# Five split pairs instead of four in the middle blocks of an attention and GeGLU kernel, with weight sums made earlier on GpSimd

## Chip, core and metric

The kernel runs on one core of a Trainium2 chip. The engines are TensorE (matmuls), VectorE (DVE), ScalarE (ACT), GpSimd (POOL) and SyncE (SP, which issues DMAs). The metric is the device time of one execution in microseconds; the median of three runs stands for a kernel.

## What is computed

For each of 8 batches, linear attention over 8 heads, 576 tokens and 64 values per head; its output, 4608 rows of 512, goes through a GeGLU layer of 1536 hidden columns:

```python
q_s = softmax(q, axis=-1); k_s = softmax(k, axis=2)
kv  = einsum('bhsd,bhse->bhde', k_s, v)
x   = einsum('bhsd,bhde->bhse', q_s, kv)      # then (B*S, H*D)
out = (gelu(x @ w_gate) * (x @ w_val)) @ w_out
```

All arrays are float32 outside; the matmuls use float16 operands and add up in float32.

## The kernel before

**Blocks.** Each batch gives a block of 512 rows; the 64 rows left over in each batch are gathered (`xtr`) into a ninth block. The order is 0 to 6, then block 8 (the gathered rows), then block 7 (`order`, L531). While TensorE works on the gate and value products of one block, the other engines do the softmax of the next batch, and DMAs load the one after.

**Plain tiles.** The 1536 hidden columns are 12 tiles of 128. A plain tile is 8 matmuls with 512 columns, 4 for the gate and 4 for the value, then a Gelu on ScalarE and a product on VectorE into `ht`. In the middle blocks `half` (L620) does the gate or the value of one tile.

**Pairs.** Tiles k and k+3 can be done together by a scheme of seven products in place of eight (Strassen's, in Winograd's form): the contraction, the tiles and the rows are halved, and sums of weights (`sum_wgv`, L580) and of x (`sum_x`, L589) replace some operands. A product is 4 matmuls of 256 columns. `pair_step` (L630) does a pair k in four steps, written k.1 to k.4:

- k.1: product 1 into bank `pa`; ScalarE copies `pa` into bank `pb`; product 5 into bank `pc`; a snapshot s5 of `pc`, on ScalarE, or on VectorE in the last two blocks (`snap`).
- k.2: product 6 on top of `pa`, snapshot s2 on ScalarE; product 3 on top of `pc`; VectorE adds `pc` and s2 into buffer `cc` (`add`).
- k.3: product 7 on top of `pa`, VectorE adds `pa` and s5 into `cc`; product 2 on top of `pb`; a half Gelu on ScalarE and a half product on VectorE write the lower half of tile k (`final`); `upper` puts a Gelu over half of `cc` on ScalarE, and GpSimd multiplies into the upper halves of tiles k and k+3 (L653).
- k.4: product 4 on top of `pa`, then `final` for the lower half of tile k+3.

The eight PSUM banks are handed out in a ring. In blocks from 3 on, pairs take two `cc` buffers in turn; in block 2 one buffer serves all.

**The written order.** The order within a block is written out by hand as strings (L611 to L615): `1.2` is a step of a pair, `8g` a half, and letters are work that rides along (`ride`, from `plan`): `a` and `n` start the softmax sums of the next batch's q (VectorE reductions; GpSimd products with `a`), `m` is two more GpSimd products of that softmax (L250), `t` transposes by DMA, `l` loads, `s0`, `s1`, `u0`, `u1` are sums of `ht` (`sum_h`, L566) for the next stage, `w` and `x` sums of weights for pair 6. Each engine runs its instructions in the order in which this code emits them. Block 2 has three pairs (`THREE`), blocks 3 to 6 have four (`FOUR`: 0, 6, 1, 2), blocks 8 and 7 all six (`SIX`). A function put into `live["late"]` is emitted after the next step.

**Out product.** `out_strassen` (L728) multiplies `ht` with `w_out` in the same way, from block 1 on: seven products of 12 matmuls with 256 columns, with the last step .4 of the block's last pair inside product 1. Sums of `w_out` (`tw`) and of `ht` (`sh`) lie in six buffers of a pool `wstp`, which first staged the float32 weights: these buffers have 2048 float16 places each, of which the sums use 1536.

**Weight sums.** Those of pairs 0 to 2 are made in blocks 0 and 1, those of pair 6 in block 2 on GpSimd, those of pairs 7 and 8 by VectorE in the out products of blocks 3, 4 and 6 (L999).

Of the kernel before, what the change touches and what calls it, by code (L numbers as in the profile page):

```python
# [9 lines left out]
f32 = mybir.dt.float32  # L10
f16 = mybir.dt.float16
# [7 lines left out]
def kernel(  # L19
# [12 lines left out]
    B, H, S, D = q.shape  # L32
    C = H * D
    F = moe_w_gate.shape[1]
    P = 128
    HP = H // 2
    NFI = F // P
# [11 lines left out]
    NO = NFI // 2  # L49
# [3 lines left out]
    wstp = ctx.enter_context(tc.tile_pool(name="wstp", bufs=6))  # L53
    att = ctx.enter_context(tc.tile_pool(name="att", bufs=2))
    ffn = ctx.enter_context(tc.tile_pool(name="ffn", bufs=4))
# [49 lines left out]
    ek_b, eq_b, v16_b = [], [], []  # L105
# [7 lines left out]
    ws = {(nm, 0): const.tile([P, 3, 2, NO // 2 * P], f16, name=f"ws{nm}") for nm in "gv"}  # L113
# [7 lines left out]
    for i, nm in enumerate("gv"):  # L121
        n = 3 * NO * P
        ws[(nm, 1)] = kt1[:, i * n:(i + 1) * n].rearrange("p (s c f) -> p s c f", s=3, c=2)
    cc_b = eq_b[1].rearrange("p n c -> p (n c)").bitcast(f32)[:, 0:1024].rearrange(
        "p (i t r) -> p i t r", i=2, t=2)

    xs_b = [xs, ld_b["v"][0].rearrange("p h x -> p (h x)").bitcast(f16)[:, 0:2048].rearrange(
        "p (i c r) -> p i c r", i=4, c=2)]
# [44 lines left out]
    wst = {}  # L173
# [373 lines left out]

    tw = {}  # L550

    def sum_w(i, eng="dve"):
        t = wstp.tile([P, NO, 256], f16, name=f"tw{i}", tag="wst")
        b11, b12 = wo_sb[:, 0:NO, 0:256], wo_sb[:, 0:NO, 256:512]
        b21, b22 = wo_sb[:, NO:NFI, 0:256], wo_sb[:, NO:NFI, 256:512]
        a, b = {1: (b12, b11), 2: (b22, tw.get(1)), 3: (b22, b12), 4: (b21, tw.get(2))}[i]
        (nc.gpsimd if eng == "pool" else nc.vector).tensor_tensor(out=t, in0=a, in1=b, op=ALU.subtract)
        tw[i] = t

    sh = {}  # L560

    def make_s():
        for i in (1, 2):
            sh[i] = wstp.tile([P, NO, 256], f16, name=f"sh{i}", tag="wst")

    def sum_h(j0, j1, which, eng="dve"):  # L566
        step = 1 if j1 - j0 == 2 else NO // 2
# [9 lines left out]

    def sum_wgv(nm, i, k=0, n=NO // 2, eng="dve"):  # L580
        w = wg_sb if nm == "g" else wv_sb
        lo, hi = slice(k * P, (k + n) * P), slice((k + NO // 2) * P, (k + NO // 2 + n) * P)
        a11, a21, a12, a22 = w[:, 0:2, lo], w[:, 0:2, hi], w[:, 2:4, lo], w[:, 2:4, hi]
        t = [ws[(nm, k // NO)][:, j, :, k % NO * P:(k % NO + n) * P] for j in range(3)]
        o, a, b, op = {1: (t[0], a21, a22, ALU.add), 2: (t[1], t[0], a11, ALU.subtract),
                       3: (a21, a11, a21, ALU.subtract), 4: (t[2], a12, t[1], ALU.subtract)}[i]
        (nc.gpsimd if eng == "pool" else nc.vector).tensor_tensor(out=o, in0=a, in1=b, op=op)
# [6 lines left out]

    def product_gv(i, ps, xt, k, first):
        lo, hi = slice(k * P, (k + 1) * P), slice((k + NO // 2) * P, (k + NO // 2 + 1) * P)
        sl = slice(k % NO * P, (k % NO + 1) * P)
        xs = xs_b[xt is st.get((B - 1, "xt"))]
        for t, w, nm in ((0, wv_sb, "v"), (1, wg_sb, "g")):
            ss = ws[(nm, k // NO)]  # L600
            for c in range(2):
                a = {1: w[:, c, lo], 2: w[:, 2 + c, lo], 3: ss[:, 2, c, sl], 4: w[:, 2 + c, hi],
                     5: ss[:, 0, c, sl], 6: ss[:, 1, c, sl], 7: w[:, c, hi]}[i]
                x = {1: xt[:, c, 0:256], 2: xt[:, 2 + c, 0:256], 3: xt[:, 2 + c, 256:512],
                     4: xs[:, 3, c], 5: xs[:, 0, c], 6: xs[:, 1, c], 7: xs[:, 2, c]}[i]
                nc.tensor.matmul(ps[:, t], a, x, start=(first and t == 0 and c == 0), stop=(c == 1),  # L606
                                 skip_group_check=True)

    THREE = ("a 6g l 6v 0.1 9g 0.2 9v w 0.3 7g 0.4 n m 1.1 t 7v 1.2 10g 1.3 s0 10v 1.4 2.1 u0 8g 2.2 8v"  # L611
             " 2.3 s1 11g u1 2.4 11v x")
    FOUR = ("a 7g l 7v n 0.1 6.1 0.2 6.2 0.3 6.3 m 10g 0.4 6.4 1.1 t 10v 1.2 s0 8g u0 1.3 8v 1.4 2.1"
            " 11g s1 2.2 11v 2.3")
    SIX = ("0.1 6.1 0.2 6.2 0.3 6.3 0.4 1.1 6.4 7.1 s0 1.2 7.2 1.3 u0 7.3 1.4 2.1 7.4 8.1 2.2"  # L615
           " 8.2 2.3 s1 8.3 2.4")
    steps = {b: (SIX if b >= B - 1 else THREE if b == 2 else FOUR).split() for b in range(2, B + 1)}
    live = {}

    def half(b, xt, c, nm):  # L620
# [9 lines left out]
    def pair_step(b, xt, k, i):  # L630
        def final(ps, fi):
            gl = ffn.tile([P, 256], f32, name="glq", tag="gl")
            nc.scalar.activation(out=gl, in_=ps[:, 1], func=ACTF.Gelu)  # L633
            nc.vector.scalar_tensor_tensor(out=ht[:, fi, 0:256], in0=ps[:, 0], scalar=_H_SCALE,  # L634
                                           in1=gl, op0=ALU.mult, op1=ALU.mult)
            let_go(ps)

        def snap(ps, dve=False):
            sn = ffn.tile([P, 2, 256], f32, name="snq", tag="snq")
            if dve:  # L640
                nc.vector.tensor_scalar(out=sn, in0=ps, scalar1=_H_SCALE, scalar2=None, op0=ALU.mult)
            else:
                nc.scalar.activation(out=sn, in_=ps, func=ACTF.Copy, scale=_H_SCALE)  # L643
            return sn

        def add(o, ps, sn):
            nc.vector.scalar_tensor_tensor(out=o, in0=ps, scalar=_H_SCALE, in1=sn,
                                           op0=ALU.mult, op1=ALU.add)

        def upper(cc):  # L650
            nc.scalar.activation(out=cc[:, :, 1], in_=cc[:, :, 1], func=ACTF.Gelu,  # L651
                                 scale=1.0 / _H_SCALE)
            (nc.vector if k == NFI - NO // 2 - 1 else nc.gpsimd).tensor_tensor(  # L653
                out=ht[:, k:k + NO // 2 + 1:NO // 2, 256:512], in0=cc[:, :, 0], in1=cc[:, :, 1],
                op=ALU.mult)

        if i == 1:
            live["odd"] = odd = b > 2 and not live.get("odd", True)
            cc = cc_b if odd else ffn.tile([P, 2, 2, 256], f32, name="cc", tag="cc", bufs=1)
            pa = big([P, 2, 256], f32, "pga", True)  # L660
            product_gv(1, pa, xt, k, True)
            pb = big([P, 2, 256], f32, "pgb", True, True)
            nc.scalar.copy(out=pb, in_=pa)  # L663
            pc = big([P, 2, 256], f32, "pgc", True)
            product_gv(5, pc, xt, k, True)
            live[k] = [cc, pa, pb, pc, snap(pc, b >= B - 1)]
            return
        cc, pa, pb, pc, s5 = live[k]
        if i == 2:
            product_gv(6, pa, xt, k, False)  # L670
            s2 = snap(pa)
            product_gv(3, pc, xt, k, False)
            add(cc[:, 0], pc, s2)
            let_go(pc)
        elif i == 3:
            product_gv(7, pa, xt, k, False)
            add(cc[:, 1], pa, s5)
            product_gv(2, pb, xt, k, False)
            final(pb, k)
            if k == NFI - NO // 2 - 1:  # L680
                live["late"] = lambda: upper(cc)
            else:
                upper(cc)
        else:
            product_gv(4, pa, xt, k, False)
            if steps[b] and steps[b][0].endswith(".1"):
                live["late"] = lambda: final(pa, k + NO // 2)
            else:
                final(pa, k + NO // 2)
# [38 lines left out]
    def out_strassen(b, last):  # L728
        yo = [yop.tile([P, 2, C], f32, name="yo", tag="yo") for _ in range(2)]
        c = (slice(0, 256), slice(256, 512))  # L730
# [31 lines left out]
        four = 2 < b < B - 1  # L762
# [3 lines left out]
            pair_step(b, get_x(b), NO // 2 - 1, 4)  # L766
            product(1, ps["a"], False, js=js[cut:4])
        ride(b, NS, 0)
        if four:
            ride(b, PR, "u1")  # L770
        if b >= B - 1:
            pair_step(b, get_x(b), NFI - NO // 2 - 1, 4)
        get("b")
# [1 line left out]
        if b > 1:  # L775
            s1 = snap("a", True)
        ride(b, PR, "e")
        sum_h(*last_js(b), (1,))
        if b >= B - 1:
            ride(b, PR, "u1")  # L780
        sum_h(*last_js(b), (2,))
        if b < 2:
# [138 lines left out]
    def at(b, kind, i, *fns):  # L921
        plan.setdefault((b, kind, i), []).extend(fns)
# [65 lines left out]
    for b in range(2, B + 1):  # L988
        for j in range(NO // 2 - 1):
            at(b, PR, f"s{j}", L(sum_h, j, NO, (1,)))  # L990
            if j and b >= B - 1:
                at(b, PR, f"u{j}", L(sum_h, j, NO, (2, 3, 4)))
            else:
                at(b, PR, f"s{j}", L(sum_h, j, NO, (3,), "pool"))
                at(b, PR, f"u{j}", L(sum_h, j, NO, (2,)), L(sum_h, j, NO, (4,), "pool"))
    for i, xs_ in (("w", ("g1", "v1", "g2", "v2")), ("x", ("g4", "v4", "g3", "v3"))):
        for x in xs_:
            at(2, PR, i, L(sum_wgv, x[0], int(x[1]), NO, 1, "pool"))
    for b, i, x in ((3, 2, "g1"), (3, 2, "g2"), (4, 2, "v1"), (4, 2, "v2"), (6, 1, "g4"), (6, 1, "v4"),  # L999
                    (6, 2, "g3"), (6, 2, "v3")):  # L1000
        at(b, NS, i, L(sum_wgv, x[0], int(x[1]), NO + 1, 2))


    def ride(b, kind, i):
        for fn in plan.get((b, kind, i), []):
            fn()
# [63 lines left out]
```

## Time and profile before

| | us |
|---|---|
| median of three runs | 293.66 (293.64 to 293.77) |
| the profiled execution | 293.74 |
| its span, first to last instruction | 292.0 |
| TensorE busy | 282.8 (97%) |
| VectorE busy | 221.8 (76%) |
| ScalarE busy | 194.9 (67%) |
| GpSimd busy | 200.5 (69%) |

Granted clock of TensorE: 1.00 throughout. The stages as TensorE's order in time gives them, in us from the span's start:

| block | gate and value products | out product |
|---|---|---|
| 1 | up to 70.85 | 70.85 to 81.82 |
| 2 | 81.82 to 101.36 | 101.36 to 112.29 |
| 3 | 112.29 to 131.10 | 131.10 to 142.31 |
| 4 | 142.31 to 161.10 | 161.10 to 172.30 |
| 8 | 232.74 to 250.77 | from 250.77 |

In the lines further on, a row of instructions in order of time has its start, the time it spans, the engine, the line of the code, the operation, what it writes and reads, the shapes and a count; in square brackets is the idle time of the engine before it and what ended it. Where a pair's `cc` lies in the memory of `eq`, the trace calls it `eq`. A matmul's end is modelled, so the pace of TensorE is read from the starts.

### The profile page before, as it was taken

What the parts mean: (1) busy time and instruction counts of PE and PEld (TensorE: products, weight loads), DVE (VectorE), ACT (ScalarE), POOL (GpSimd) and SP (SyncE); (2) the same over time, 40 slices, a digit from 0 to 9 for tenths busy, and PEclk for the clock granted to TensorE, in tenths of its full rate; (3) what the DMA queues carried; (4) which work ended last, traced back from release to release, by engine and by line L of the source; (5) the groups of instructions that cost most, each with busy time, mean ns of one, the idle gap of its engine ahead of it and who ended that gap; (6) DMA issues with size and microseconds to landing.
All of it is one profiled execution on the core that took longest, in us unless ns stands there. A gap on an engine that the chain in (4) does not pass through costs nothing.

```text
span 292.0 us, 6352 instructions
## 1 busy us (share of the span) xinstructions
PE 282.8 (97%) x2449; PEld 203.1 (70%) x2449; DVE 221.8 (76%) x412; ACT 194.9 (67%) x322; POOL 200.5 (69%) x187
## 2 busy tenths in 40 slices
PE   3999999999999999999999999999999999999994
PEld 1544446445866687778776878687868888888883
DVE  2854789878878768677967897687868879938992
ACT  3773367785786578758986798669864577537650
POOL 1567846970489799877888688869895576283640
PEclk9999999999999999999999999999999999999999
DMA  6999999998059704990299019901141110033003
GB/s 215 374 381 388 401 391 390 357 342 237 4 175 387 160 3 144 356 221 3 114 341 283 3 74 326 318 6 74 73 77 26 72 74 0 3 72 75 0 2 144
DMA packets 54622, 51.72 MB, mean 177 GB/s; under 512 B 18496, under 2 KB 50496, under 8 KB 54592
## 3 DMA queue, kind: packets, MB, share of 16 engines
q1 hardware_dynamic: 52864, 49.49, 53.5%
q10 hardware_dynamic: 1728, 1.84, 2.0%
q8 instruction: 19, 0.31, 0.4%
q14 instruction: 11, 0.09, 0.1%
HBM read 37.75 MB, written 9.44 MB: 162 GB/s over the span
## 4 chain that ended last, share of the span: by engine, by line
PE 94%; DVE 2%; DMA 2%; ACT 0%; issue 0%; ACTq 0%
PE pga L606 19%; PE psa L718 15%; PE psg L467 14%; PE psv L467 14%; PE pgc L606 9%; PE psc L718 7%; PE pgb L606 5%; PE psb L718 4%; PE psy L535 4%; DMA qt<-in_q_dram 2%; PE pskv L343 2%; PE psx L430 1%; DVE rq L240 1%; PE psx L409 1%; DVE eq L250 0%; PE pskv L284 0%
## 5 line engine op out<-in xcount | busy, mean ns | idle before, releaser
L467 PE MATMUL psg<-xt,wg_sb 128*128 128x512 f16 x184 | 49.3, 379 | 0.0
L467 PE MATMUL psv<-xt,wv_sb 128*128 128x512 f16 x184 | 49.2, 379 | 0.0
L250 POOL TENSOR_TENSOR eq<-eq,rrq 128x640 f16<-128x640 f16 (+1 forms) x27 | 34.7, 1303 | 11.8 <-DVE rrq L242 8.2
L718 PEld LDWEIGHTS <-ht 128*128 128x128 f16 x384 | 36.6, 98 | 7.6 <-issue 2.5
L606 PEld LDWEIGHTS <-wv_sb 128*128 128x128 f16 x248 | 24.1, 98 | 9.4 <-issue 1.0
L467 PEld LDWEIGHTS <-wv_sb 128*128 128x128 f16 x184 | 17.9, 98 | 18.0 <-issue 0.8
L653 POOL TENSOR_TENSOR ht<-eq 128x512 f16<-128x512 f32 x14 | 17.8, 1273 | 18.1 <-ACT eq L651 18.1
L467 PEld LDWEIGHTS <-wg_sb 128*128 128x128 f16 x184 | 17.9, 98 | 16.5
L576 POOL TENSOR_TENSOR s<-ht,sh 128x512 f16<-128x512 f16 x19 | 22.4, 1178 | 9.8 <-DVE sh L576 9.8
L634 DVE SCALAR_TENSOR_TENSOR ht<-pga,glq 128x256 f16<-128x256 f32 x31 | 13.1, 423 | 20.7 <-ACT glq L633 20.6
L188 POOL CAST v<-vt 128x640 f16<-128x640 f32 x26 | 18.7, 761 | 12.8 <-PE pskv L343 11.3
L576 POOL TENSOR_TENSOR ht<-ht 128x512 f16<-128x512 f16 x19 | 23.1, 1215 | 6.1 <-DVE sh L576 6.1
L606 PEld LDWEIGHTS <-wg_sb 128*128 128x128 f16 x248 | 24.2, 98 | 2.8
L653 POOL TENSOR_TENSOR ht<-cc 128x512 f16<-128x512 f32 x15 | 19.5, 1303 | 8.5 <-ACT cc L651 8.5
L472 ACT ACTIVATE gl<-psg 128x512 f32<-128x512 f32 x24 | 13.8, 598 | 16.7 <-PE psg L467 16.7
L633 ACT ACTIVATE glq<-pgb 128x256 f32<-128x256 f32 x31 | 11.7, 379 | 18.7 <-PE pgb L606 10.9
L718 PE MATMUL psa<-tw,ht 128*128 128x256 f16 x192 | 23.4, 272 | 0.1
L473 DVE SCALAR_TENSOR_TENSOR ht<-psv,gl 128x512 f16<-128x512 f32 x24 | 16.1, 688 | 9.5 <-PE psv L467 7.6
L212 ACT ACTIVATE ek<-kt 128x1280 f16<-128x1280 f32 (+1 forms) x11 | 19.1, 1748 | 5.5 <-DMA kt<-in_k_dram 3.9
L663 ACT COPY pgb<-pga 128x512 f32<-128x512 f32 x31 | 18.0, 580 | 6.7 <-PE pga L606 6.4
L643 ACT ACTIVATE snq<-pga 128x512 f32<-128x512 f32 x31 | 18.5, 600 | 4.0 <-PE pga L606 3.7
L240 DVE TENSOR_REDUCE rq<-eq 128x20 f32<-128x1280 f16 (+1 forms) x12 | 17.2, 1432 | 4.6 <-ACT eq L212 4.6
(172 smaller groups left out, 729.6 us busy)
## 6 DMA issues: line engine op xcount, KB each, us to landing
out_dram<-yo SPq DMA_DIRECT2D x15, 512.0 KB, 3.4
kt<-in_k_dram SPq DMA_DIRECT2D x7, 640.0 KB, 9.0
vt<-in_v_dram SPq DMA_DIRECT2D x7, 640.0 KB, 5.3
qt<-in_q_dram SPq DMA_DIRECT2D x7, 640.0 KB, 7.7
qt<-in_q_dram SPq DMA_DIRECT2D x8, 512.0 KB, 7.8
wost<-in_moe_w_out_dram SPq DMA_DIRECT2D x6, 512.0 KB, 7.9
kt<-in_k_dram SPq DMA_DIRECT2D x6, 512.0 KB, 9.5
vt<-in_v_dram SPq DMA_DIRECT2D x6, 512.0 KB, 5.8
```

Source lines behind the costliest of these rows:

```text
L188: nc.gpsimd.tensor_copy(out=dst, in_=src)
L212: nc.scalar.activation(out=dst[:, n0:NC, h0 * D:h1 * D].rearrange(o, d=D, **({"t": 2} if b >= QUAD else {})), in_=heads(tiles[(nm, b)], b, ...
L240: nc.vector.reduce_sum(rq, e, axis=mybir.AxisListType.X)
L250: (nc.gpsimd if eng == "pool" else nc.vector).tensor_tensor(out=e, in0=e, in1=rrq.unsqueeze(-1).to_broadcast((P, n, 2, D)), op=ALU.mult)
L467: nc.tensor.matmul(ps, w[:, ci, fi * P:(fi + 1) * P], xt[:, ci, :], start=(ci == 0), stop=(ci == HP - 1))
L473: nc.vector.scalar_tensor_tensor(out=ht[:, fi, :], in0=psv, scalar=_H_SCALE, in1=gl, op0=ALU.mult, op1=ALU.mult)
L576: (nc.gpsimd if eng == "pool" else nc.vector).tensor_tensor(out=o, in0=a, in1=b, op=op)
L606: nc.tensor.matmul(ps[:, t], a, x, start=(first and t == 0 and c == 0), stop=(c == 1), skip_group_check=True)
L643: nc.scalar.activation(out=sn, in_=ps, func=ACTF.Copy, scale=_H_SCALE)
L653: (nc.vector if k == NFI - NO // 2 - 1 else nc.gpsimd).tensor_tensor(out=ht[:, k:k + NO // 2 + 1:NO // 2, 256:512], in0=cc[:, :, 0], in1=c ...
L663: nc.scalar.copy(out=pb, in_=pa)
L718: nc.tensor.matmul(ps[t], a, w, start=(first and j == js[0] and (t == ts[0] or ps[t].tensor is not ps[ts[0]].tensor)), stop=(j == js[-1]), ...
```

## The change

The strings are replaced. Block 2 has pairs 0, 1, 7, 2 (`FOUR`), blocks 3 to 6 pairs 0, 6, 1, 7, 2 (`FIVE`); tiles 8 and 11 stay plain there. In block 2 pairs too take two `cc` buffers in turn, the second in the memory of the other `eq`. In blocks 3 to 6 the snapshot s5 of pairs 1 and 7 goes to VectorE, and `upper` is put off to after the next step for every pair but pair 2. The sums of `ht` for j=1 in these blocks come all in the out product, and all on VectorE; before, two of them were GpSimd's. The weight sums of pair 7 and most of those of pair 8 are made by GpSimd in block 1, and lie in the last 512 places of the six buffers of `wstp`; two small ones follow in block 6.

```diff
-    THREE = ("a 6g l 6v 0.1 9g 0.2 9v w 0.3 7g 0.4 n m 1.1 t 7v 1.2 10g 1.3 s0 10v 1.4 2.1 u0 8g 2.2 8v"
-             " 2.3 s1 11g u1 2.4 11v x")
-    FOUR = ("a 7g l 7v n 0.1 6.1 0.2 6.2 0.3 6.3 m 10g 0.4 6.4 1.1 t 10v 1.2 s0 8g u0 1.3 8v 1.4 2.1"
-            " 11g s1 2.2 11v 2.3")
+    FOUR = ("a 6g l 6v 0.1 9g 0.2 9v w 0.3 1.1 0.4 n m 7.1 1.2 t 7.2 1.3 s0 7.3 1.4 2.1 u0 7.4 8g 2.2 8v"
+            " 2.3 s1 11g u1 2.4 11v x")
+    FIVE = ("a 8g l 8v n 0.1 6.1 0.2 6.2 0.3 6.3 m 0.4 1.1 6.4 7.1 t 1.2 7.2 s0 1.3 7.3 u0 2.1 1.4 11g 2.2"
+            " 7.4 11v 2.3 s1")
...
-    steps = {b: (SIX if b >= B - 1 else THREE if b == 2 else FOUR).split() for b in range(2, B + 1)}
+    steps = {b: (SIX if b >= B - 1 else FOUR if b == 2 else FIVE).split() for b in range(2, B + 1)}
...
-            live["odd"] = odd = b > 2 and not live.get("odd", True)
-            cc = cc_b if odd else ffn.tile([P, 2, 2, 256], f32, name="cc", tag="cc", bufs=1)
+            live["odd"] = odd = not live.get("odd", True)
+            cc = cc_b[b > 2] if odd else ffn.tile([P, 2, 2, 256], f32, name="cc", tag="cc", bufs=1)
...
-            live[k] = [cc, pa, pb, pc, snap(pc, b >= B - 1)]
+            live[k] = [cc, pa, pb, pc, snap(pc, b >= B - 1 or b > 2 and k % NO == 1)]
...
-            if k == NFI - NO // 2 - 1:
+            if k == NFI - NO // 2 - 1 or 2 < b < B - 1 and k != 2:
                 live["late"] = lambda: upper(cc)
...
-        if four:
-            ride(b, PR, "u1")
...
-        if b >= B - 1:
+        if b > 2:
             ride(b, PR, "u1")
...
-            if j and b >= B - 1:
+            if j and b > 2:
                 at(b, PR, f"u{j}", L(sum_h, j, NO, (2, 3, 4)))
...
-    for b, i, x in ((3, 2, "g1"), (3, 2, "g2"), (4, 2, "v1"), (4, 2, "v2"), (6, 1, "g4"), (6, 1, "v4"),
-                    (6, 2, "g3"), (6, 2, "v3")):
-        at(b, NS, i, L(sum_wgv, x[0], int(x[1]), NO + 1, 2))
+    for kind, i, xs_, n in ((FI, 6, ("g1", "v1", "g2"), 2), (FI, 9, ("v2", "g4", "v4"), 2), (NS, 0, ("g3", "v3"), 1)):
+        for x in xs_:
+            at(1, kind, i, L(sum_wgv, x[0], int(x[1]), NO + 1, n, "pool"))
+    for x in "gv":
+        at(6, NS, 1, L(sum_wgv, x, 3, NO + 2, 1, "pool"))
```

The rest of the diff gives the six buffers their longer shape and lets the weight sums of pairs 7 and 8 be found in them:

```diff
+    def wst16(name, key):
+        t = wstp.tile([P, NO * 256 + 512], f16, name=name, tag="wst")
+        ws78[key] = t[:, NO * 256:].rearrange("p (c f) -> p c f", c=2)
+        return t[:, 0:NO * 256].rearrange("p (j c) -> p j c", j=NO)
...
+    def w_sum(nm, j, k, n=1):
+        if k > NO:
+            return ws78[(nm, j)][:, :, (k - NO - 1) * P:(k - NO - 1 + n) * P]
+        return ws[(nm, k // NO)][:, j, :, k % NO * P:(k % NO + n) * P]
```

More of the change, by code (lines that the diff above doesn't have):

```diff
@@ L123 @@
         ws[(nm, 1)] = kt1[:, i * n:(i + 1) * n].rearrange("p (s c f) -> p s c f", s=3, c=2)
-    cc_b = eq_b[1].rearrange("p n c -> p (n c)").bitcast(f32)[:, 0:1024].rearrange(
-        "p (i t r) -> p i t r", i=2, t=2)
+    cc_b = [x.rearrange("p n c -> p (n c)").bitcast(f32)[:, 0:1024].rearrange(
+        "p (i t r) -> p i t r", i=2, t=2) for x in eq_b]
     xs_b = [xs, ld_b["v"][0].rearrange("p h x -> p (h x)").bitcast(f16)[:, 0:2048].rearrange(
@@ L546, in store @@
                                   ap=[[pm, nm], [NM * pn, 2]] + last), in_=src)
-    tw = {}
+    tw, ws78 = {}, {}
+    def wst16(name, key):
+        t = wstp.tile([P, NO * 256 + 512], f16, name=name, tag="wst")
+        ws78[key] = t[:, NO * 256:].rearrange("p (c f) -> p c f", c=2)
+        return t[:, 0:NO * 256].rearrange("p (j c) -> p j c", j=NO)
     def sum_w(i, eng="dve"):
-        t = wstp.tile([P, NO, 256], f16, name=f"tw{i}", tag="wst")
+        t = wst16(f"tw{i}", (None, ("g", 0), ("v", 0), ("g", 1), ("v", 1))[i])
         b11, b12 = wo_sb[:, 0:NO, 0:256], wo_sb[:, 0:NO, 256:512]
@@ L563, in make_s @@
         for i in (1, 2):
-            sh[i] = wstp.tile([P, NO, 256], f16, name=f"sh{i}", tag="wst")
+            sh[i] = wst16(f"sh{i}", (None, ("g", 2), ("v", 2))[i])
     def sum_h(j0, j1, which, eng="dve"):
@@ L583, in sum_wgv @@
         a11, a21, a12, a22 = w[:, 0:2, lo], w[:, 0:2, hi], w[:, 2:4, lo], w[:, 2:4, hi]
-        t = [ws[(nm, k // NO)][:, j, :, k % NO * P:(k % NO + n) * P] for j in range(3)]
+        t = [w_sum(nm, j, k, n) for j in range(3)]
         o, a, b, op = {1: (t[0], a21, a22, ALU.add), 2: (t[1], t[0], a11, ALU.subtract),
@@ L596, in product_gv @@
         lo, hi = slice(k * P, (k + 1) * P), slice((k + NO // 2) * P, (k + NO // 2 + 1) * P)
-        sl = slice(k % NO * P, (k % NO + 1) * P)
         xs = xs_b[xt is st.get((B - 1, "xt"))]
         for t, w, nm in ((0, wv_sb, "v"), (1, wg_sb, "g")):
-            ss = ws[(nm, k // NO)]
             for c in range(2):
-                a = {1: w[:, c, lo], 2: w[:, 2 + c, lo], 3: ss[:, 2, c, sl], 4: w[:, 2 + c, hi],
-                     5: ss[:, 0, c, sl], 6: ss[:, 1, c, sl], 7: w[:, c, hi]}[i]
+                a = {1: w[:, c, lo], 2: w[:, 2 + c, lo], 4: w[:, 2 + c, hi], 7: w[:, c, hi]}.get(i)
+                if a is None:
+                    a = w_sum(nm, {3: 2, 5: 0, 6: 1}[i], k)[:, c]
                 x = {1: xt[:, c, 0:256], 2: xt[:, 2 + c, 0:256], 3: xt[:, 2 + c, 256:512],
```

## The prediction

> **What bounds the kernel now.** I read the page's slices first, then the engines' busy time by stretch (column order: start and end, length, then busy us and count for each engine, granted clock, DMA share, GB/s), then the orders in time of TensorE, GpSimd and VectorE.
>
> ```profile
> PE   3999999999999999999999999999999999999994
> ...
> 101.36:112.29 10.93, 10.93 (x141) 8.80 (x140) 7.32 (x14) 8.07 (x8) 10.93 (x14) 1.00 0.01 2
> 112.29:131.10 18.81, 18.81 (x142) 13.68 (x140) 14.35 (x27) 13.88 (x28) 16.68 (x14) 1.00 0.92 280
> ```
>
> TensorE is busy without a break from the tenth microsecond on, at full clock; VectorE, ScalarE and GpSimd have a quarter, a quarter and a tenth of block 3's first part (112.29 to 131.10) left. Busy matmuls can hide a slow pace, so I look at the starts:
>
> ```profile
> 119.29 1.03 PE L467 MATMUL psg<-xt,wg_sb 128*128 128x512 f16 x4
> 120.15 0.38 PE L606 MATMUL pga<-xs,wv_sb 128*128 128x256 f16 x2
> 120.37 0.38 PE L606 MATMUL pga<-xs,wg_sb 128*128 128x256 f16 x2
> ```
>
> Four matmuls of 512 columns advance TensorE by 120.15-119.29 = 0.86 us, two of 256 by 0.22. All stretches keep this pace: TensorE streams, and every other engine is just in time. So a matmul less shortens the kernel, and a wait of TensorE lengthens it by its full length. How near "just in time" is shows in block 3's GpSimd and VectorE:
>
> ```profile
> 116.72 2.49 POOL L250 TENSOR_TENSOR eq<-eq,rrq 128x640 f16<-128x640 f16 x2
> 119.98 1.28 POOL L653 TENSOR_TENSOR ht<-eq 128x512 f16<-128x512 f32 x1 [0.77 <-ACT eq L651]
> 121.21 1.28 POOL L653 TENSOR_TENSOR ht<-cc 128x512 f16<-128x512 f32 x1
> 122.44 2.49 POOL L250 TENSOR_TENSOR eq<-eq,rrq 128x640 f16<-128x640 f16 x2
> ...
> 119.49 0.68 DVE L647 SCALAR_TENSOR_TENSOR cc<-pga,snq 128x512 f32<-128x512 f32 x1
> ```
>
> GpSimd multiplies the upper halves of pairs 0 and 6 (L653) first, and then the two softmax products of item m (L250, 2.49 us together).
>
> And block 8, which already runs six pairs:
>
> ```profile
> 243.43 0.68 DVE L647 SCALAR_TENSOR_TENSOR eq<-pga,snq 128x512 f32<-128x512 f32 x1
> ...
> 244.17 0.38 PE L606 MATMUL pga<-xs,wv_sb 128*128 128x256 f16 x2
> ```
>
> Step 1.4 (product 4 into pga) starts 0.06 us after the add that reads the same pga ends (244.11). That is a wait met with nothing to spare, in a block without softmax work.
>
> **What the Trainium skill says.** "PSUM — Partial Sum Buffer", Engine vs sequencer instructions: the queues of ScalarE, VectorE and GpSimd are strict first in, first out. The trace agrees: GpSimd idles 0.77 us before L653 at 119.98 although item m could run (its reciprocals ended at 116.91). "TensorE: Matmul & The Clock Gate", Step-by-step: 512 columns back to back take about 216 ns; here 0.86/4. "SBUF — State Buffer", SBUF: two separate sides: VectorE and GpSimd take a shared port pair by an exclusive lock. The trace agrees: a VectorE sum (L576) beside GpSimd sums took 0.96 us at 103.75, 0.42 elsewhere.
>
> **The change, part by part.**
>
> *Matmuls.* A pair is 28 matmuls of 256 columns: 28 x 0.1094 = 3.06 us. The two tiles it replaces are 16 of 512: 16 x 0.216 = 3.46. One pair more in each of blocks 2 to 6: 5 x 0.40 = 2.0 us less TensorE time. That is the whole gain.
>
> *Work added.* A pair costs ScalarE one copy, two snapshots, two half Gelus, one upper Gelu: 0.58+0.60+0.60+0.38+0.38+0.63 = 3.17 us, against two Gelus of 0.60. VectorE: two adds of 0.69 and two products of 0.42 = 2.2, against two of 0.68. In blocks 3 to 6 two snapshots of 0.69 come over from ScalarE, and two sums of 0.42 from GpSimd. So VectorE gains 0.9+1.4+0.8 = 3.1 us a block, ScalarE 0.8.
>
> *Weight sums.* Six GpSimd sums of 512 and two of 256 elements enter block 1. GpSimd idles there for 11.34 us (65.3 to 76.66). The 512 form on weights is not shown: L593, the same shape, gives 1.15 each (8.2 us in all with two of 0.67); doubling the slowest 256 form (0.85) gives 1.7 (11.5 in all). I take 8.5; even 11.5 only delays casts of v that are not read until 102. VectorE sums beside it may lose 0 to 0.5 us each by the lock; they end at 72.74 and product 5 needs the first (72.28) at 73.47, so I take nothing. A gain is excluded, since TensorE has no gap there. The eight VectorE sums that go from blocks 3, 4 and 6 (0.82 each in block 3) stood beside out-product matmuls and are worth nothing; the two 0.67 sums left in block 6 fall in GpSimd's idle stretch. No DMA is added; the transpose behind item m is issued no later.
>
> *The order in blocks 3 to 6.* I walk block 3 with the durations above, starts following each other by 0.60 (VectorE 512), 0.33 (256 and sums), 0.50 (ScalarE), 1.23 (GpSimd); a PSUM result is readable 0.70 us after its product's first matmul (117.98 to 118.68), any other hand-over takes 0.07. TensorE's new starts follow from the step lengths (0.875 for steps .1 to .3, 0.44 for step .4, 0.865 for half a tile): 0.4 at 119.29, 1.1 at 119.73, 6.4 at 120.60, 7.1 at 121.04, 1.2 at 121.92, 7.2 at 122.79, 1.3 at 123.67, 7.3 at 124.54, 2.1 at 125.42, 1.4 at 126.29. Up to step 6.3 nothing moves but the upper Gelu of pair 0: it is queued behind pair 6's half Gelu, ending on ScalarE at 120.45. GpSimd multiplies it from 120.52 to 121.8. Now item m comes next in its queue (the postponed upper of pair 6 is emitted after step 0.4, behind m): 121.75 to 124.2. Then pair 6's upper, 124.2 to 125.48.
>
> Two VectorE instructions need that: the first add of pair 7, which writes the cc buffer of pair 6 (two buffers alternate), and sum s0, which reads pair 6's upper half. The add could start at 124.15: its product 3 is readable at 123.93, and its snapshot s2 runs on ScalarE from 123.49 to 124.09, as ScalarE is level with TensorE there (pair 1's copy 120.88, pair 7's 121.74, s2 of pair 1 at 122.62). It starts at 125.55. Behind it in VectorE's queue: s0 at 126.15, and pair 1's second add, 126.48 to 127.16. Step 1.4 overwrites that bank; TensorE is there at 126.29 and waits until 127.22: 0.9 us. PSUM banks are not the limit: pair 2 takes the two that pairs 0 and 6 gave back by 123.3, and pair 1's third.
>
> The backlog goes on. ScalarE's upper of pair 1 needs that add, and pair 2's copy and snapshots stand behind it: s2 ends at 130.67, just when TensorE wants product 7 (130.70). VectorE then has add, product, tile 11's product and pair 2's second add in a row from 130.73: that last ends at 132.94. Step 2.4, inside the out product, is reached at 131.62+0.66 = 132.28 and waits until 133.0: 0.7 us. The rest is one more waiting gap of 0.04. Later sums keep clear (first sum for product 5 near 135.9 against 136.2). Net per block: 0.9+0.7-0.4 = +1.2. Bounds: first wait 0.6 to 1.2 (its ends are GpSimd rows of small spread); second 0 to 1.1 (a chain of some fifteen instructions). Blocks 4 to 6 show the same GpSimd order within 0.2 us, so four times: +4.8.
>
> *Block 2.* Upper Gelus stay immediate, but item n puts 1.48+0.28 us of reductions into VectorE's queue just before pair 1's adds, with pair 7's add now between. Walked likewise: n from 90.84 to 92.55, adds at 92.55, 93.15 and 93.75, the last ending 94.43; step 1.4 is reached at 93.75 (0.16 of it small waits for ScalarE) and waits 0.7. At the end 0.2 before product 7 of pair 2, 0.2 before 2.4. Sum 1.3-0.4 = +0.9 (0 to 1.3).
>
> Sum: 0.9 + 4.8 = +5.7. The profiled execution took 293.74 (span 292.0 and 1.7 around it; 0.08 over the median of 293.66): 293.7+5.7 = 299.4.
>
> **Rivals.** *The queues keep up (faster).* The matmul sum alone: 293.7-2.0 = 291.7. For it: block 8 runs six pairs without a TensorE wait, and GpSimd idles 1.3 us before 120.52. It decides at one place, the first add of pair 7: if GpSimd has finished pair 6's upper by 124.5, the chain of 0.60+0.33+0.68 ends before 126.23 and step 1.4 never waits. Against it: m's 2.49 us stand in front, and I get 125.48. (Without that delay the same row of four VectorE instructions ends at 131.57, and step 2.4, due at 131.31, still waits 0.3 a block: 292.9 belongs to this case too.) *Only the first wait is real.* The tail is absorbed by ScalarE and VectorE catching up while TensorE stands: 0.9-0.4 = +0.5 a block and +0.4 in block 2, 296.2. *Even.* Waits of 0.4 a block eat the gain, 293.7. *Worse.* Late upper halves of pair 2 also hold product 5 in the out part, 0.6 a block more: 302.
>
> **How the numbers follow.** Forecast 0.60 (297.5 to 301.2), first wait only 0.20 (294.4 to 297.5), faster 0.10, even 0.04, worse 0.06. A range of 295.0 to 301.5 holds the first, most of the second and a piece of the last, about 0.79. A change below 0.2% (0.6 us) can't be told from none here: faster 0.10, same 0.04, slower 0.86.
>
> **What would show it.** Right: L653 of pair 6 behind the two L250 of item m; VectorE idle before an L647 with GpSimd as releaser, 1.4 us, in blocks 3 to 6; TensorE gaps at steps 1.4 and 2.4; a block over 31 us instead of 30.0; no gap in block 1. Wrong: TensorE still without gaps and blocks of 29.6 us, or gaps in the out products waiting for sums.

## The result, and the profile after

The changed kernel takes 301.76 us (median of four runs, 301.69 to 301.89), against 293.7 before: a ratio of 1.0275 with a 95% interval of 1.0257 to 1.0293. The forecast was 299.4, its range ended at 301.5: the way was right, the loss was 8.1 us and not 5.7. The span went from 292.0 to 300.0 us. TensorE's order in time tells where:

| block | from start to start, before | after | lost | forecast |
|---|---|---|---|---|
| up to the start of block 2 | 81.82 | 83.55 | 1.73 | 0 |
| 2 | 30.47 | 31.88 | 1.41 | 0.9 |
| 3 | 30.02 | 31.22 | 1.20 | 1.2 |
| 4, 5, 6 together | 90.43 | 93.89 | 3.46 | 3.6 |
| 8, 7 and the end | 59.3 | 59.5 | 0.2 | 0 |

TensorE's row of the page's slices is no help: a 9 stands for 90% of 7.5 us or more, so waits of half a microsecond hardly show in it (one digit has become an 8, that of the slice from 67.5 to 75.0):

```profile
PE   3999999998999999999999999999999999999994
```

The chain of waits does show them. First its line by engine before the change, then after it:

```profile
PE 94%; DVE 2%; DMA 2%; ACT 0%; issue 0%; ACTq 0%
```

```profile
PE 71%; DVE 11%; POOL 8%; issue 4%; ACT 4%; ACTq 1%; DVEq 0%; POOLq 0%
```

TensorE's own work was the path before; now VectorE, GpSimd and ScalarE make up almost a quarter of it. That is their share of the path and not time lost: TensorE is busy during most of it. How much is lost, and where, the orders in time tell.

TensorE in blocks 1 and 3:

```profile
72.17 1.26 PE L728 MATMUL psb<-wo_sb,ht 128*128 128x256 f16 x10
74.85 0.39 PE L728 MATMUL psb<-wo_sb,ht 128*128 128x256 f16 x2 [1.42 <-DVE ht L473]
...
129.22 0.38 PE L616 MATMUL pgc<-xs,wsg 128*128 128x256 f16 x2
130.32 0.38 PE L616 MATMUL pga<-xs,wv_sb 128*128 128x256 f16 x2 [0.72 <-DVE cc L657]
...
134.68 0.82 PE L728 MATMUL psa<-wo_sb,ht 128*128 128x256 f16 x6
136.12 0.38 PE L616 MATMUL pga<-xs,wv_sb 128*128 128x256 f16 x2 [0.62 <-DVE cc L657]
```

By the starts, at a pace of 0.109 us a matmul, the first wait of block 3 (step 1.4) is 130.32-129.44 = 0.88 us and the second (step 2.4) 136.12-135.34 = 0.78. The wait in block 1, inside product 2, is 1.6 us by this pace (74.85-73.26); it is the one that the forecast did not have.

Block 3's GpSimd, then its VectorE, of the changed kernel:

```profile
123.67 1.27 POOL L663 TENSOR_TENSOR ht<-cc 128x512 f16<-128x512 f32 x1 [1.32 <-ACT cc L661]
124.90 2.48 POOL L250 TENSOR_TENSOR eq<-eq,rrq 128x640 f16<-128x640 f16 x2
127.34 1.26 POOL L663 TENSOR_TENSOR ht<-eq 128x512 f16<-128x512 f32 x1
```

```profile
126.39 0.69 DVE L657 SCALAR_TENSOR_TENSOR cc<-pgc,snq 128x512 f32<-128x512 f32 x1
128.64 0.69 DVE L657 SCALAR_TENSOR_TENSOR eq<-pgc,snq 128x512 f32<-128x512 f32 x1 [1.56 <-POOL ht L663]
129.25 0.41 DVE L582 TENSOR_TENSOR sh<-ht 128x512 f16<-128x512 f16 x1
129.58 0.68 DVE L657 SCALAR_TENSOR_TENSOR cc<-pga,snq 128x512 f32<-128x512 f32 x1
```

The two softmax products of item m (L250) stand between the upper halves of pair 0 and pair 6 (L663). Pair 7's first add (128.64) comes after 1.56 us in which VectorE waits for pair 6's upper half, and pair 1's second add (129.58), which step 1.4 needs, stands behind it. Block 3 starts 3.14 us later than before; with that, the forecast's times for the second upper half (124.2) and for the add (125.55) become 127.34 and 128.69, and the trace has 127.34 and 128.64.

Now block 1: VectorE's sums and tile 11's product before the change, then after it, then GpSimd after it:

```profile
65.63 0.42 DVE L576 TENSOR_TENSOR sh<-sh,ht 128x512 f16<-128x512 f16 x1
66.91 0.42 DVE L576 TENSOR_TENSOR s<-ht,sh 128x512 f16<-128x512 f16 x1
...
71.12 0.69 DVE L473 SCALAR_TENSOR_TENSOR ht<-psv,gl 128x512 f16<-128x512 f32 x1 [0.37 <-PE psv L467]
```

```profile
65.64 1.26 DVE L582 TENSOR_TENSOR sh<-sh,ht 128x512 f16<-128x512 f16 x1
66.83 0.68 DVE L473 SCALAR_TENSOR_TENSOR ht<-psv,gl 128x512 f16<-128x512 f32 x1
67.43 0.77 DVE L582 TENSOR_TENSOR ht<-ht 128x512 f16<-128x512 f16 x1
68.12 1.37 DVE L582 TENSOR_TENSOR s<-ht,sh 128x512 f16<-128x512 f16 x1
...
74.12 0.68 DVE L473 SCALAR_TENSOR_TENSOR ht<-psv,gl 128x512 f16<-128x512 f32 x1
```

```profile
65.30 1.32 POOL L598 TENSOR_TENSOR tw<-wg_sb 128x512 f16<-128x512 f16 x1
66.58 1.33 POOL L598 TENSOR_TENSOR tw<-wv_sb 128x512 f16<-128x512 f16 x1
67.88 1.33 POOL L598 TENSOR_TENSOR tw<-tw,wg_sb 128x512 f16<-128x512 f16 x1
```

VectorE's float16 sums take 0.66 to 1.37 us beside GpSimd's weight sums, 0.42 before. The product that reads PSUM (L473) keeps its 0.68. The sums don't idle, they run longer: the first long one ends at 66.90, 0.28 us after the GpSimd sum that was running when it started (66.62), and the second at 69.49, again 0.28 after one (69.21). Seven sums run longer, by 4.1 us together; VectorE makes up 1.1 us of that in gaps that it had before, and tile 11's product starts at 74.12 in place of 71.12, 3.0 us late. TensorE waits for it.

### The profile page after: what moved, and what is told of

Read it like the earlier page. It is cut to its first block, busy times and chain, and to the rows that moved or that the text cites. A ratio compares the mean times of both kernels' runs of the same rounds, so it can differ in the third digit from the quotient of the medians.

```text
span 300.0 us, 6549 instructions
## 1 busy us (share of the span) xinstructions
PE 283.3 (94%) x2509; PEld 208.5 (70%) x2509; DVE 229.5 (76%) x430; ACT 198.3 (66%) x334; POOL 205.9 (69%) x194
## 4 chain that ended last, share of the span: by engine, by line
PE 71%; DVE 11%; POOL 8%; issue 4%; ACT 4%; ACTq 1%; DVEq 0%; POOLq 0%
PE pga L616 14%; PE psa L728 13%; PE psg L467 7%; PE psc L728 7%; PE pgc L616 7%; PE psv L467 6%; PE psy L535 3%; POOL ht L663 3%; POOL eq L250 3%; PE psb L728 3%; PE pgb L616 3%; PE pswarm L459 2%; DVE cc L657 2%; DVE ht L473 2%; DVE eq L657 2%
## 5 line engine op out<-in xcount | busy, mean ns | idle before, releaser
L250 POOL TENSOR_TENSOR eq<-eq,rrq 128x640 f16<-128x640 f16 (+1 forms) x27 | 34.7, 1302 | 12.1 <-DVE rrq L242 8.3
L467 PE MATMUL psg<-xt,wg_sb 128*128 128x512 f16 x144 | 39.0, 379 | 0.0
L467 PE MATMUL psv<-xt,wv_sb 128*128 128x512 f16 x144 | 38.9, 379 | 0.0
L663 POOL TENSOR_TENSOR ht<-cc 128x512 f16<-128x512 f32 x18 | 22.9, 1274 | 21.2 <-ACT cc L661 21.0
L616 PE MATMUL pga<-xs,wv_sb 128*128 128x256 f16 x120 | 22.9, 272 | 6.3 <-DVE eq L657 3.2
L582 POOL TENSOR_TENSOR s<-ht,sh 128x512 f16<-128x512 f16 x15 | 17.3, 1155 | 15.2 <-DVE sh L582 13.7
L663 POOL TENSOR_TENSOR ht<-eq 128x512 f16<-128x512 f32 x16 | 20.7, 1292 | 8.4 <-ACT eq L661 8.2
L673 ACT COPY pgb<-pga 128x512 f32<-128x512 f32 x36 | 20.9, 582 | 4.1 <-PE pga L616 3.8
L653 ACT ACTIVATE snq<-pga 128x512 f32<-128x512 f32 x36 | 21.5, 601 | 3.0 <-PE pga L616 2.7
L616 PE MATMUL pga<-xs,wg_sb 128*128 128x256 f16 x120 | 22.9, 272 | 0.0
L582 POOL TENSOR_TENSOR ht<-ht 128x512 f16<-128x512 f16 x15 | 17.3, 1154 | 6.8 <-DVE sh L582 6.8
L473 DVE SCALAR_TENSOR_TENSOR ht<-psv,gl 128x512 f16<-128x512 f32 x24 | 16.0, 684 | 7.7 <-PE psv L467 5.8
```

Of the source, the lines that this page charges most:

```text
L467: nc.tensor.matmul(ps, w[:, ci, fi * P:(fi + 1) * P], xt[:, ci, :], start=(ci == 0), stop=(ci == HP - 1))
L473: nc.vector.scalar_tensor_tensor(out=ht[:, fi, :], in0=psv, scalar=_H_SCALE, in1=gl, op0=ALU.mult, op1=ALU.mult)
```

## The experiments

Two theories run through them. Theory 1: the loss is one of order and contention, from single instructions that stand in the wrong place. The rival: five pairs add more work to VectorE and ScalarE than these can hold, in whatever order.

**Without the weight sums.**

```diff
         if k > NO:
-            return ws78[(nm, j)][:, :, (k - NO - 1) * P:(k - NO - 1 + n) * P]
+            return ws[(nm, 0)][:, j, :, (k - NO) * P:(k - NO + n) * P]
...
-            at(1, kind, i, L(sum_wgv, x[0], int(x[1]), NO + 1, n, "pool"))
...
-        at(6, NS, 1, L(sum_wgv, x, 3, NO + 2, 1, "pool"))
```

> The changed kernel without the weight sums of pairs 7 and 8: these pairs read the sums of pairs 1 and 2 in their place, so the output is another one; matmuls, order and all else stay. Theory 1 (GpSimd's weight sums slow VectorE's sums in block 1 until tile 11's product is late): the 1.42 us wait in block 1's product 2 goes, blocks 2 to 6 stay as they are, about 300.0 us. Rival (the sums are innocent, block 1 is late from a dependence through the lengthened buffers, which stay): 301.7.

299.96 us. Block 1's wait is gone (block 2 starts at 81.76), and block 3 keeps its waits (0.73 and 0.62 in the brackets). So block 1's loss comes from these sums and from nothing else that was changed; the buffers were as long here.

**The sums added to the kernel before.**

```diff
+    for i, xs_ in ((6, ("g1", "v1", "g2")), (9, ("v2", "g4", "v4"))):
+        for x in xs_:
+            at(1, FI, i, L(sum_78, x[0], int(x[1])))
```

(`sum_78` is `sum_wgv` for pairs 7 and 8 together, into the spare places.)

> The kernel before, with only the six large weight sums of 512 elements added on GpSimd in block 1, in the spare quarters; nothing reads them. Theory 1 (contention of GpSimd and VectorE): VectorE's L576-type sums between 65 and 73 us go from 0.42 to 0.7 to 1.3 us each, TensorE waits about 1.2 us in block 1's product 2, 294.7 to 295.1 us, other blocks unchanged. Rival (block 1's wait needs the new pairs or the two small sums that rewrite the weights): 293.7.

294.88 us, ratio 1.0039 (1.0024 to 1.0053). TensorE waits in the same place and nowhere else, and block 2 starts 1.20 us later:

```profile
74.32 0.39 PE L732 MATMUL psb<-wo_sb,ht 128*128 128x256 f16 x2 [0.94 <-DVE ht L473]
```

VectorE's sums have the same lengths as in the changed kernel (1.26, 0.78, 1.37, 0.66, 1.26, 0.78), though nothing reads GpSimd's. They take longer, with no idle time before them, and the run without the weight sums had the long buffers and no wait: it is contention of the two engines and not a dependence through the buffers. The remaining 0.5 us of block 1 in the changed kernel fit the two small sums that rewrite the weights, which lengthen one more sum (0.89 at 73.31, against 0.41 here).

**Copies in their place.** The edit is against the kernel of the last run.

```diff
-        nc.gpsimd.tensor_tensor(out=o, in0=a, in1=b, op=op)
+        copy_on("pool", o, a)
+        copy_on("pool", o, a)
```

> The kernel before with twelve GpSimd copies of 512 float16 elements in block 1, two in the place of each of the six sums of the other run. Theory 1a (any GpSimd instruction on SBUF shuts VectorE's float16 sums out): the sums between 65 and 73 us lengthen as with the sums, a wait in product 2 of 0.3 to 1.0 us, 294.0 to 294.8 us. Theory 1b (only instructions with two inputs do): sums stay near 0.42 us, 293.6 to 293.8.

294.22 us, ratio 1.0022 (1.0012 to 1.0032). Block 1's out product takes 11.48 us, 10.97 before. Copies of 512 elements, of about 0.7 us each, lengthen VectorE's sums to 0.71 to 0.82 us. The wait is not in product 2, where it was expected, but in product 6, which writes the bank that VectorE reads late (0.34 us by pace):

```profile
74.97 1.49 PE L733 MATMUL psa<-tw,sh 128*128 128x256 f16 x12 [0.18 <-DVE sn L765]
```

So one input is enough. GpSimd is busy for as long as with the sums (65.1 to 73.6 us, against 65.2 to 73.0), in instructions of half the length, and tile 11's product on VectorE falls 1.4 us behind in place of 2.5, counted from the start of the out product. This fits a loss that grows with the length of the GpSimd instruction that a sum runs into. Copies have one input less, too; but the two-input sums of half the length, further on, also lengthen VectorE's sums by less (to 0.77 to 0.91 us).

**Item m later.**

```diff
-    FIVE = ("a 8g l 8v n 0.1 6.1 0.2 6.2 0.3 6.3 m 0.4 1.1 6.4 7.1 t 1.2 7.2 s0 1.3 7.3 u0 2.1 1.4 11g 2.2"
+    FIVE = ("a 8g l 8v n 0.1 6.1 0.2 6.2 0.3 6.3 0.4 m 1.1 6.4 7.1 t 1.2 7.2 s0 1.3 7.3 u0 2.1 1.4 11g 2.2"
```

> The changed kernel with item m put behind step 0.4 in blocks 3 to 6, so that GpSimd multiplies pair 6's upper half before the two softmax products. Theory 1 (that half is late because m stands before it): VectorE's wait for GpSimd and TensorE's wait at step 1.4 (0.7 to 0.9 us) go, the wait at 2.4 shrinks to about 0.3; blocks of 29.9 to 30.0 us instead of 31.2; about 296.8 us in all. Rival (VectorE simply has 3 us more work in a block, and any order leaves it late): waits move elsewhere, over 300.5 us.

298.63 us: 3.1 us gained, between the two expectations. The order in time says why. The upper half of pair 6 now comes first, and VectorE waits no more for it:

```profile
124.87 1.27 POOL L663 TENSOR_TENSOR ht<-eq 128x512 f16<-128x512 f32 x1
126.10 2.49 POOL L250 TENSOR_TENSOR eq<-eq,rrq 128x640 f16<-128x640 f16 x2
```

```profile
127.24 0.69 DVE L657 SCALAR_TENSOR_TENSOR eq<-pgc,snq 128x512 f32<-128x512 f32 x1 [0.18 <-ACT snq L653]
127.84 1.03 DVE L582 TENSOR_TENSOR sh<-ht 128x512 f16<-128x512 f16 x1
...
133.05 0.69 DVE L657 SCALAR_TENSOR_TENSOR cc<-pgc,snq 128x512 f32<-128x512 f32 x1 [0.60 <-POOL s L582]
```

```profile
129.56 0.63 ACT L661 ACTIVATE cc<-cc 128x512 f32<-128x512 f32 x1 [0.40 <-DVE cc L657]
...
132.36 0.61 ACT L653 ACTIVATE snq<-pga 128x512 f32<-128x512 f32 x1
```

The wait at step 1.4 fell from 0.88 to 0.11 us. The one at 2.4 stayed (0.77): item m now runs beside sum s0, which takes 1.03 us in place of 0.41. Pair 1's second add comes later by as much, ScalarE idles 0.40 us before the upper Gelu of pair 1, which needs it, and six instructions further on in ScalarE's queue the snapshot s2 of pair 2 ends at 132.97; pair 2's first add starts 0.08 us later (133.05). The trace names a GpSimd sum as what ended this add's wait, but in the next run the same add starts (132.88) while that sum still runs. So theory 1 holds for the first wait, and not for the second, which it had shrinking to 0.3. A block takes 30.45 us, still over the 30.0 of before.

**Upper Gelus at once.**

```diff
-            if k == NFI - NO // 2 - 1 or 2 < b < B - 1 and k != 2:
+            if k == NFI - NO // 2 - 1:
```

> The changed kernel with the upper Gelus of blocks 3 to 6 emitted at once again, as before; item m where the change has it. Theory 1 (what counts is that GpSimd multiplies pair 6's upper half before item m): the wait at 1.4 goes as with m moved, the one at 2.4 stays near 0.6, 298.4 to 298.9 us. Rival (moving m helped by itself, through its transposes or through VectorE's lock): first wait stays, over 301 us.

298.21 us. The same relief by another edit, so it is the place of pair 6's upper half relative to m that counts, and not m's own. Step 1.4 has no gap and s0 takes 0.48 here; but the upper Gelus of pairs 1 and 7 now both stand before pair 2's copy on ScalarE, and product 6 of step 2.2 waits 0.41 us for that (0.24 in the trace's bracket). The wait at 2.4 is only 0.28, in part because TensorE comes there 0.41 us later. A block takes 30.3 us.

**Step 7.4 moved (with m later).**

```diff
-            " 7.4 11v 2.3 s1")
+            " 11v 2.3 7.4 s1")
```

> Item m behind step 0.4 as in the second run, and besides step 7.4 moved from before tile 11's value half to after step 2.3, which gives VectorE one product less before pair 2's second add and TensorE 0.44 us more work. Theory 1 (the wait at 2.4 is the queue of VectorE between snapshot s2 and that add): the 0.62 us waits at 2.4 go in blocks 3 to 6, blocks of 29.7 us, 296.1 us. Rival (the wait is set by ScalarE or GpSimd, so that the row only shifts): it stays at 0.4 or more, 297.6 to 298.6.

301.37 us: a miss, as bad as the change itself. No wait at 2.4, but two others: TensorE reaches product 7 of pair 2 before its snapshot (0.30 us in the bracket), and the last matmuls of product 1 wait for the product behind step 2.4, since VectorE now does the product of 7.4 and sum s1 first:

```profile
133.02 0.38 PE L616 MATMUL pga<-xs,wv_sb 128*128 128x256 f16 x2 [0.30 <-ACT snq L653]
...
137.69 0.39 PE L728 MATMUL psa<-wo_sb,ht 128*128 128x256 f16 x2 [0.80 <-DVE ht L644]
```

The wait at 2.4 went, as theory 1 said, but the delay was handed to what follows. Two things changed at once (one product less ahead of VectorE's add, 0.44 us more work for TensorE before 2.4), so this run does not tell which of them took the wait away.

**Five pairs with small early sums.** Block 2 with three pairs as before; only pair 7's weight sums in block 1, as sums of 256 elements, after tile 6; pair 8's on VectorE later, as before; FIVE as in the last run.

```diff
+    for x in ("g1", "v1", "g2", "v2", "g4", "v4"):
+        at(1, FI, 6, L(sum_wgv, x[0], int(x[1]), NO + 1, 1, "pool"))
+    for x in "gv":
+        at(2, NS, 2, L(sum_wgv, x, 3, NO + 1, 1))
```

> The version that theory 1 proposes: five pairs in blocks 3 to 6 with m behind 0.4 and 7.4 behind 2.3; block 2 with three pairs as before; only pair 7's weight sums early, as six of 256 elements on GpSimd in block 1 and two on VectorE in block 2's out product; pair 8's on VectorE later, as before. Theory 1: four blocks of 29.7 instead of 30.0 us, block 1 late by 0 to 0.4 us: 292.2 to 292.8 us, faster than before. Rival (the added work of VectorE and ScalarE cancels the matmuls in any order): 293.6 or more.

297.90 us, another miss: it has the last run's order, and its waits in each block (0.30 and 0.80 again; 31.1 us a block). What it tells is block 1: block 2 starts at 81.76, with six GpSimd sums of half the length, so the slack of block 1 holds those.

**Uppers last.** The same early sums; m and 7.4 where the change has them; the upper Gelus of pairs 0 and 6 at once, that of pair 1 behind step 2.1, that of pair 7 behind step 2.2 (`y` emits the next one that was put off).

```diff
-    FIVE = ("a 8g l 8v n 0.1 6.1 0.2 6.2 0.3 6.3 m 0.4 1.1 6.4 7.1 t 1.2 7.2 s0 1.3 7.3 u0 2.1 1.4 11g 2.2"
-            " 7.4 11v 2.3 s1")
+    FIVE = ("a 8g l 8v n 0.1 6.1 0.2 6.2 0.3 6.3 m 0.4 1.1 6.4 7.1 t 1.2 7.2 s0 1.3 7.3 2.1 y u0 1.4 11g 2.2"
+            " y 7.4 11v 2.3 s1")
...
-            if k == NFI - NO // 2 - 1 or 2 < b < B - 1 and k != 2:
+            if k == NFI - NO // 2 - 1:
                 live["late"] = lambda: upper(cc)
+            elif 2 < b < B - 1 and k % NO == 1:
+                live.setdefault("up", []).append(lambda: upper(cc))
```

> As the version with small early sums (block 2 with three pairs, pair 7's weight sums alone early), but with the change's places for m and 7.4, the upper Gelus of pairs 0 and 6 at once, those of pairs 1 and 7 behind pair 2's copy and snapshots s5 and s2 on ScalarE. Theory 1 (the wait at the end of the gate and value part is pair 2's snapshot s2 standing behind these Gelus in ScalarE's queue, then VectorE's queue): s2 0.5 to 0.8 us earlier, waits of 0.2 us or less per block, 292.3 to 293.2 us, faster than before. Rival (VectorE's and ScalarE's added work cancels the matmuls in any order): 293.7 to 295.

292.17 us, ratio 0.9954 (0.9944 to 0.9963): faster than before. The four blocks take 29.65, 29.63, 29.64 and 29.86 us, with a gap of 0.10 at 2.4 as the only wait. ScalarE's order shows pair 2's copy and snapshots ahead of the Gelus:

```profile
126.26 0.57 ACT L675 COPY pgb<-pga 128x512 f32<-128x512 f32 x1
126.74 0.60 ACT L655 ACTIVATE snq<-pgc 128x512 f32<-128x512 f32 x1
127.23 0.63 ACT L663 ACTIVATE eq<-eq 128x512 f32<-128x512 f32 x1
```

In blocks 3 to 6 the order differs from that of the run with the upper Gelus at once only by where those of pairs 1 and 7 stand. Snapshot s2 of pair 2 ends 16.62 us after the start of block 3, 17.43 there, and the wait at 2.4 and that of product 6 are gone: the tail is a matter of ScalarE's queue. So the fifth pair does fit: the rival, that its work cancels the matmuls in any order, has fallen for blocks 3 to 6.

**The same, with sum s0 behind step 7.3.**

```diff
-    FIVE = ("a 8g l 8v n 0.1 6.1 0.2 6.2 0.3 6.3 m 0.4 1.1 6.4 7.1 t 1.2 7.2 s0 1.3 7.3 2.1 y u0 1.4 11g 2.2"
+    FIVE = ("a 8g l 8v n 0.1 6.1 0.2 6.2 0.3 6.3 m 0.4 1.1 6.4 7.1 t 1.2 7.2 1.3 7.3 s0 2.1 y u0 1.4 11g 2.2"
```

> The same with sum s0 behind step 7.3, so that pair 1's second add does not stand behind it. Theory 1: within 0.4 us of the last, a little faster if the add comes earlier (292.2 to 293.0 us). Rival: as there, 293.7 or more.

294.58 us, 2.4 us more: a miss for theory 1. The time lies in the rival's range, but the work is that of the last run and only one sum has moved, so it is again the order. It is the mechanism of the change once more, with other parts. GpSimd's sum that follows s0 now starts at 127.10 and stands before pair 1's upper half; pair 2 writes the `cc` buffer of pair 1, and its first add waits for it:

```profile
128.39 1.27 POOL L665 TENSOR_TENSOR ht<-eq 128x512 f16<-128x512 f32 x1
```

```profile
129.69 0.69 DVE L659 SCALAR_TENSOR_TENSOR eq<-pgc,snq 128x512 f32<-128x512 f32 x1 [1.35 <-POOL ht L665]
```

TensorE then waits 0.71 us at 2.4 in each block.

**Item n of block 2 earlier.**

```diff
-    FOUR = ("a 6g l 6v 0.1 9g 0.2 9v w 0.3 1.1 0.4 n m 7.1 1.2 t 7.2 1.3 s0 7.3 1.4 2.1 u0 7.4 8g 2.2 8v"
+    FOUR = ("a 6g l 6v n 0.1 9g 0.2 9v w 0.3 1.1 0.4 m 7.1 1.2 t 7.2 1.3 s0 7.3 1.4 2.1 u0 7.4 8g 2.2 8v"
```

> The changed kernel with item n of block 2 moved from behind step 0.4 to before step 0.1, where VectorE was idle for 1.8 us. Theory 1 (n's 1.75 us of reductions stand in VectorE's queue before pair 1's adds): the waits at 1.4 (0.55 us) and 7.4 (0.19 us) of block 2 go, the later ones shrink; 300.7 to 301.0 us. Rival (block 2 is late from ScalarE and GpSimd, n only passes time): 301.6 to 301.8.

301.34 us: 0.4 gained, about half of what theory 1 said, and between the two ranges. The wait at 1.4 fell from 0.71 to 0.23 us by pace, but at 7.4 it grew from 0.35 to 0.54: s0 takes 1.00 us there, beside item m on GpSimd, and VectorE's adds wait for ScalarE's snapshots instead (1.12 us idle). So n is only a part of block 2's delay; GpSimd and ScalarE, which the rival named, have a part in it too.

**Four pairs in block 2, on the fastest version.**

```diff
+    FOUR = ("a 6g l 6v n 0.1 9g 0.2 9v w 0.3 1.1 0.4 m 7.1 8g 1.2 t 7.2 1.3 s0 7.3 2.1 y u0 1.4 8v 2.2"
+            " y 7.4 11g 2.3 s1 11v u1 2.4 x")
```

> The version with uppers last, and four pairs in block 2 as well: n before step 0.1, tile 8's halves between 7.1 and 1.2 and between 1.4 and 2.2, upper Gelus of pairs 1 and 7 put off as in blocks 3 to 6; pair 7's two small rewriting sums back on GpSimd in block 1. Theory 1 (block 2's waits come from what stands in ScalarE's and VectorE's queues at 7.1 to 1.4, not from the pair's work itself): waits of 0.3 us or less in block 2, 0.1 to 0.4 us faster than that version, 291.8 to 292.1 us. Rival (block 2, with GpSimd at nine tenths, has no room for a fourth pair): 292.4 to 293.5.

292.55 us against 292.17 for three pairs, each with its own runs of the kernel before (ratios 0.9957 and 0.9954, intervals of about 0.1% on either side): no gain. The time lies in the rival's range, though both expectations hold in part. The gate and value part of block 2 has no gap left, so its waits were a matter of order. But the out product waits 0.71 us by pace for a GpSimd sum that comes too late:

```profile
108.79 0.39 PE L730 MATMUL psc<-wo_sb,s 128*128 128x256 f16 x2 [0.55 <-POOL s L582]
```

That eats the 0.40 of the fourth pair: block 2 takes 30.63 us, and 30.52 with three. GpSimd is without a gap from 101.06 on there. In this order block 2 has no room for a fourth pair. The two other orders with four pairs, the change's and that with n earlier, took longer still (31.88 and 31.57).

## Why the prediction went wrong

**TensorE's sum.** Right: the version with almost no waits has blocks of 29.63 us where they were 30.07, 0.4 less for each pair.

**The order in blocks 3 to 6.** Right in mechanism, place and size: pair 6's upper half behind item m, VectorE idle for 1.56 us before pair 7's add (1.4 forecast), waits of 0.88 and 0.78 us (0.9 and 0.7), 4.7 us over four blocks (4.8). Two runs with different edits took the first wait away.

**The tail.** Right in size and in cause. With 3.14 us added, the forecast has snapshot s2 of pair 2 end at 133.81 and pair 2's second add at 136.08; the trace has 133.77 and 136.07. Only the aside, that without the first delay 2.4 would still wait 0.3 us, did not hold for the order that took the delay away by moving m: there it waited 0.77, since s0 then ran beside GpSimd and took 1.03 us, where the walk had 0.42.

**Block 2.** A term too small: 1.41 and not 0.9. The wait at 1.4 was as forecast (0.7). At 7.4 no wait was forecast and 0.35 came, again behind a sum (s0) that took 0.82 us in place of 0.42; the two later ones were 0.2 and 0.3. The lengthened sums are missing from this term too.

**Weight sums in block 1: the step that failed.** It said: "VectorE sums beside it may lose 0 to 0.5 us each by the lock; they end at 72.74 and product 5 needs the first (72.28) at 73.47, so I take nothing." Two things were wrong in it. The bound was read off one row (0.96 at 103.75), and "0.42 elsewhere" does not hold even before the change: the next sum took 0.77 (104.74), and in the out products of blocks 3 to 6 one took 1.26, a loss of 0.84:

```profile
134.73 1.26 DVE L576 TENSOR_TENSOR sh<-sh,ht 128x512 f16<-128x512 f16 x1
```

In block 1 single sums lost up to 0.95 us. The losses were also not added up: seven sums lost 4.1 us, and VectorE, already busy for four fifths of that time before, could make up only 1.1 of that and was 3.0 us late. And the slack was looked for at the wrong consumer: the sums share VectorE's queue with the products of the tiles, and product 2 needs tile 11's product before product 5 needs a sum. Before, that product ended at 71.81 and TensorE wanted it at about 73.3, a slack of 1.4 us; 3.0-1.4 = 1.6, and the wait came out at 1.6. The page of the skill that was quoted ("SBUF — State Buffer", SBUF: two separate sides: an exclusive lock, held for the whole instruction) had it right, and the trace agrees (sums that end 0.28 us after the GpSimd instruction they met); the pricing did not follow. The sign "no gap in block 1" failed.

With 1.7 for block 1 in the sum, the forecast would have been 301.1 us; most of the rest is block 2. The rival "worse" named 302, close to the measured time, but for another cause: product 5 of the out products in blocks 3 to 6 does not wait for late sums, so its number came near by chance.

## What to carry to other kernels

A buffer that is handed round between engines ties the writer to the queue of the last reader: before a slow engine's instruction is put off, ask what stands in front of it there and who writes that buffer next. Work "in an idle gap" of GpSimd isn't free for VectorE: add up what every float16 sum beside it can lose, and look for the slack in all that stands behind these sums, not in their own readers. When TensorE has no gap at all, count such delays in tenths of a microsecond for each block, and test the order: here one order of the same five pairs made a block 1.2 us longer, and another made it 0.4 us shorter.

## What was not expected of the hardware

A VectorE float16 sum of 512 elements (0.42 us alone) that meets a running GpSimd instruction ends 0.28 us after that one does: in block 1 of the changed kernel for example 66.62 and 66.90, 69.21 and 69.49, 71.80 and 72.08. Over the thirteen traces, 159 rows of a single such sum start during a single GpSimd instruction; 154 of them end 0.27 to 0.30 us after it, whether that has float16 or float32 inputs, 256 or 512 elements. In the other five both start within 0.01 us, the sum keeps its 0.42 and the GpSimd instruction takes 1.56 us in place of 1.27.

Instructions of VectorE that read PSUM and write float16 (0.68 us) showed no lengthening beside the same GpSimd sums. GpSimd pays too, but less: its weight sums of 512 elements took 1.32 to 1.34 us in block 1, and sums of that shape 1.15 where no VectorE sum ran beside them; of 256 elements, the two in block 1 took 0.84 and 0.85, those in block 6 0.67. And plain one-input copies on GpSimd lengthen VectorE's sums as well, only by less each, being shorter.
